# Numbers first, a table in two parts, fewer products of zeros, and other PSUM banks in a fused attention and two-layer kernel

## The chip, the core and the metric

The kernel runs on one core of a Trainium2 chip. The metric is the device time of one execution in microseconds, as the median of three runs. A separate execution is recorded by the hardware profiler; its own time stands beside the median below. The engines are TensorE (PE, matmuls; PEld is its weight load), VectorE (DVE), ScalarE (ACT), GpSimd (POOL) and SyncE (SP), which issues most transfers.

## The reference

Attention over a window with a distance penalty, then two feed-forward layers on the 1536 tokens:

```python
scores = scale * np.matmul(q, k.transpose(0, 1, 3, 2))       # B=2, H=8, S=768, D=64
rel = pos[:, None] - pos[None, :]
is_global = pos[None, :] < int(n_global)                     # 8
is_local = (rel >= 0) & (rel < int(n_local))                 # 96
keep = is_global | is_local
dist = np.where(is_global & ~is_local, float(n_local), np.abs(rel))
scores = np.where(keep, scores + bias, -1e9)                 # bias = -slope[head] * dist
a = softmax(scores)                                          # sum + 1e-9 below the line
x = a @ v                                                    # -> 1536 x 512
h = x @ w_in; g = where(h > 0, h, exp(min(h, 0)) - 1); x = g @ w_out          # 512-2048-512
h = max(x @ w1, x @ w2, x @ w3); out = h @ w_out                              # 512-768-512
```

All arithmetic is in fp32 accuracy. The weights come as 64-bit words that the kernel takes apart, and products run in three parts (high by high, high by low, low by high). `n_global` and `n_local` are inputs, so the table of distances is finished on the chip after they have landed.

## The kernel before

**The steps of the attention.** The work goes in steps of 128 tokens and one pair of heads, two steps to a tile `raw` of queries and keys. A step whose tokens are the first 128 of a sequence has 128 keys, every other one 232. For the first block of 512 tokens the 16 steps run in a loop of `windowed`. In pass k of that loop the following is recorded, and each engine runs its own part in this order (the schedule is manual, nothing is reordered):

- `scores_pe(k)`: PE's scores, L228, into the banks S0 and S1 (k even) or y0 and y1 (k odd)
- in some passes `fill`: products of the identity that nobody reads, L765, into bank h
- `turn_pe(k - 2)`: PE transposes the weights of step k - 2, L298 (128 keys) or L304 (232), into one bank of the ring TX, y2, y3
- `values_pe(k - 3)`: PE's product with v, L327, into the bank that holds the transposes of step k - 3
- `scores_dve(k)`: DVE adds the table of distances `rel` to the scores and takes the minimum, L254, one call per head
- `turn_act(k - 2)`, `scores_act(k)`, `values_high(k - 3)`, `sums(k)`: ACT's copy of the transposes L315, exponentials L275, high part xh L337, sums L237
- `recip(k - 1)`, `norm(k - 1)`: DVE's reciprocal L266 and scaling L288
- `values_low(k - 4)`: DVE's low part xl, L343, the last reader of that step's bank
- from pass 8 on (`CONV`) pieces of the taking apart of the weights, on DVE and ACT

**Ahead of the loop.** PE makes 10 products of zeros (`warm`, L765 with z). POOL writes positions, the scales `qsc` of the queries (8 memsets) and the identity, and scales the queries of each `raw` tile (L198). DVE turns the positions into the table: L152 to L154 before the numbers `ni` are there, L165 to L169 after. SP issues `raw` of pair 0, then `ni`, then pairs 1 and 2.

**Behind the loop.** `begin` starts the feed-forward layer. The first long product `h` is followed by a second one in the same bank, tag h, which waits until DVE's L702 has read the first. Then the outputs y, four tiles in the banks y0 to y3, get eight matmuls with the high part of the activation (`out_high`, L708) and four with the low part (`out_low`, L716). From there on the loop over 16 chunks of the hidden layer fills PE.

Of the kernel before, what the change touches and what calls it, by code (L numbers as in the profile page):

```python
# [12 lines left out]
F32 = mybir.dt.float32  # L13
# [25 lines left out]
BLOCKS = [512, 512, 512]  # L39
CONV = 8  # L40
EARLY = 28
WARM = 10
FILL = {1: 2, 2: 2, 8: 2, 9: 2, 10: 2, 11: 2, 12: 2, 13: 2}
WLOAD = 2, 5, 9, 13
CHUNKS = [(c, i) for c in range(NCC) for i in range(3)]
BEHIND = [(c, i) for c in range(NCC) for i in (0, 2)] + [(c, 1) for c in range(NCC)]
# [3 lines left out]
def load_numbers(nc, pool, n_ap):  # L50
    ni = pool.tile([P, 4], I32, name="ni")
    nc.sync.dma_start(ni, n_ap.bitcast(I32).partition_broadcast(P))
    return ni
# [63 lines left out]
class Windowed:  # L117
# [17 lines left out]
    def positions(self, scratch):  # L135

        nc, c = self.nc, self.const
        n = P + WIN
        rel = c.tile([P, n], F32, name="rel")
        key, neg = scratch[0][:, 0:n], scratch[1][:, 0:n]  # L140
        far = 1 << 20
        o = 0
        for num, step, base, cm, kstep, kbase in (
            (P, -1, 0, 1, 1, 0),
            (PREV, -1, PREV, 1, 0, far),
            (G, 0, far, 0, 1, 0),
            (P, -1, 0, 1, 0, far),
        ):
            iota(nc, rel[:, o:o + num], num, step, base, cm)
            iota(nc, key[:, o:o + num], num, kstep, kbase, 0)  # L150
            o += num
        nc.vector.tensor_scalar(neg, rel, 0.0, None, op0=ALU.is_lt)  # L152
        nc.vector.scalar_tensor_tensor(rel, rel, UNIT, neg, op0=ALU.mult, op1=ALU.max)
        nc.vector.tensor_scalar(key, key, UNIT, None, op0=ALU.mult)  # L154
        self.qsc = query_scales(nc, c, UNIT)
        self.ident = c.tile([P, P], F32, name="ident")
        make_identity(nc, self.ident)
        self.base, self.key, self.tmp = rel, key, neg

    def bases(self, ni):  # L160


        nc, rel, key, t = self.nc, self.base, self.key, self.tmp
        w = self.const.tile([P, 4], F32, name="nu")
        nc.vector.tensor_scalar(w, ni, UNIT, None, op0=ALU.mult)  # L165
        ng, nl = w[:, 0:1], w[:, 2:3]
        nc.vector.tensor_scalar(key, key, ng, nl, op0=ALU.is_ge, op1=ALU.max)
        nc.vector.scalar_tensor_tensor(t, rel, nl, rel, op0=ALU.is_ge, op1=ALU.add)
        nc.vector.tensor_tensor(rel, t, key, op=ALU.min)  # L169
# [229 lines left out]
class Feed:  # L399
# [301 lines left out]
    def elu_max(self, e, h):  # L701
        self.nc.vector.scalar_tensor_tensor(e, e, -1.0, h, op0=ALU.add, op1=ALU.max)  # L702

    def out_high(self, y, fc, g, n):
        w = self.w[fc][:, 1]
        for e in range(NCC):
            for a in range(2):
                self.nc.tensor.matmul(  # L708
                    y[e][:, 0:n], w[:, a, e * P:e * P + P], g[0][:, 0:n],
                    start=fc == 0 and a == 0, stop=False,  # L710
                )

    def out_low(self, y, fc, g, n):
        w = self.w[fc][:, 1]
        for e in range(NCC):
            self.nc.tensor.matmul(  # L716
                y[e][:, 0:n], w[:, 0, e * P:e * P + P], g[1][:, 0:n],
                start=False, stop=fc == NFC - 1,
            )
# [48 lines left out]
    def begin(self, at, k, x, h):  # L768


        copy, n = self.nc.scalar.copy, BLOCKS[0]
        at.load_values(k)
        self.w_ahead(4)
        at.turn_pe(k - 2, "y2")
        at.scores_pe(k, m=2)
        at.recip(k - 1)
        at.norm(k - 1)
        at.turn_pe(k - 1)
        e = self.elu_exp(h, n)
        self.elu_max(e, h)  # L780
        h = self.ps.tile([P, 512], F32, tag="h", name="h")
        self.product(h, self.w[1][:, 0], x, n, order=BEHIND)
        at.turn_act(k - 2, copy)
        self.c_rebase(2)
        at.scores_dve(k)
        self.c_rest(1, 1)
        self.c_low(2)
        gh = self.high(e, n)
        at.turn_act(k - 1, copy)
        at.scores_act(k)  # L790
        at.sums(k)
        self.c_word(2, 0)
        prev = gh, self.low(e, gh, n)
        at.pair_pe(k - 2)
        e = self.elu_exp(h, n)
        self.c_word(2, 1)
        self.elu_max(e, h)
        at.pair_out(k - 2, copy)
        self.c_high(2)
        y = self.out_tiles()  # L800
        self.out_high(y, 0, prev, n)
        self.out_low(y, 0, prev, n)
        at.recip(k)
        at.norm(k)
        gh = self.high(e, n)
        self.c_rebase(3)
        self.c_rest(2)
        gl = self.low(e, gh, n)
        k += 1
        at.turn_pe(k - 1)  # L810
        at.turn_act(k - 1, copy)
        at.scale_queries(k // 2 + 1)
        at.load_pair(k // 2 + 2)
        self.w_ahead(6)
        at.scores_dve(k)
        at.scores_act(k)
        at.sums(k)
        self.c_low(3)
        self.c_word(3, 0)
        at.recip(k)  # L820
        at.norm(k)
        return y, (gh, gl)
# [411 lines left out]
def windowed(tc, ctx, io, flag):  # L1234
# [4 lines left out]
    at.close = own.close  # L1239
    with tc.manual_schedule():  # L1240
        scratch = [f.cv.tile([P, 512], F32, tag="wr", name="sc") for _ in range(2)]
        at.load_pair(0, True)
        f.warm(WARM)
        at.positions(scratch)
        ni = load_numbers(nc, at.const, io["nn"])
        for p in range(1, 3):
            at.load_pair(p, True)
        at.scale_queries(0)
        at.bases(ni)
        first = BLOCKS[0] // GRP * 8  # L1250
        x = f.split_tiles()

        def convert():
            f.c_rebase(0)
            f.c_low(0)
            yield
            f.c_word(0, 0)
            f.c_rebase(1)
            yield
            f.c_word(0, 1)  # L1260
            yield
            f.c_high(0)
            f.c_low(1)
            yield
            f.c_rest(0)
            yield
            f.c_word(1, 0)
            yield
            yield
            f.c_word(1, 1, 0)  # L1270
            yield

        words = convert()
        h = f.ps.tile([P, 512], F32, tag="h", name="h")
        tags = "TX", "y2", "y3"
        for k in range(first):
            e = k % 2
            at.load_values(k, True)
            if e == 0:
                at.load_pair(k // 2 + 3, True)  # L1280
                at.scale_queries(k // 2 + 1)
            at.scores_pe(k, (("S0", "S1"), ("y0", "y1"))[e])
            if k in FILL:
                f.fill(at.ident, FILL[k])
            at.turn_pe(k - 2, tags[k % 3])
            at.values_pe(k - 3)
            if k >= first - 2:
                f.product(h, f.w[0][:, 0], x, GRP, 0, (k - first + 2) * 6, 6)
            at.scores_dve(k, True)
            at.turn_act(k - 2, nc.scalar.copy)  # L1290
            at.scores_act(k)
            at.values_high(k - 3, x)
            at.sums(k)
            at.recip(k - 1)
            at.norm(k - 1)
            at.values_low(k - 4, x)
            if k >= CONV:
                next(words, None)
            if k in WLOAD:
                f.w_load()  # L1300

        def half(first, count):
            f.product(h, f.w[0][:, 0], x, 2 * GRP, GRP, first, count, CHUNKS)

        k = first
        at.load_values(k, True)
        at.load_pair(k // 2 + 3)
        at.scale_queries(k // 2 + 1)
        at.turn_pe(k - 2, tags[k % 3])
        at.values_pe(k - 3)  # L1310
        at.recip(k - 1)
        at.norm(k - 1)
        at.turn_act(k - 2, nc.scalar.copy)
        at.values_high(k - 3, x)
        at.values_low(k - 4, x)
        f.c_word(1, 1, 1)
        f.c_high(1, 0)
        f.c_high(1, 1)
        at.scores_pe(k, m=2)
        at.turn_pe(k - 1, tags[(k + 1) % 3])  # L1320
        at.scores_dve(k, True)
        at.values_low(k - 3, x)
        at.values_pe(k - 2)
        at.turn_act(k - 1, nc.scalar.copy)
        at.values_high(k - 2, x)
        at.scores_act(k)
        at.scores_dve(k + 1, True)
        at.values_low(k - 2, x)
        f.c_rest(1, 0)
        at.values_pe(k - 1)  # L1330
        half(0, 6)
        at.values_high(k - 1, x)
        at.sums(k)
        at.values_low(k - 1, x)
        half(6, 3)
        half(9, 3)
        at.scores_act(k + 1)
        at.sums(k + 1)
        at.recip(k)
        at.norm(k)  # L1340
        for _ in words:
            pass
        begun = f.begin(at, k + 2, x, h)
        f.run(at, first + 4, x, begun, lambda: covered(nc, at.const, ni, flag))
# [100 lines left out]
```

## Time and profile before

| | |
|---|---|
| median of 3 runs | 542.40 us (542.32 to 542.52) |
| profiled execution | 542.16 us, of which the span from first to last instruction is 540.4 us |
| PE busy | 530.4 us, 98% of the span |
| DVE, ACT, POOL busy | 73%, 53%, 15% |

The span is the time between the program's first and last instruction on the core. Busy shares of PE count its matmuls with modelled ends. The views used below are the page's chain of work that ended last, the sums over stretches of time, the timelines of single engines and the list of transfers with the time from issue to landing.

### The profile page before, as it was taken

The numbers are of one execution on the slowest core, as the hardware profiler recorded it, in microseconds if no ns is written. First come the engines' busy times: TensorE is split into PE (matmuls) and PEld (weight loads), VectorE is DVE, ScalarE is ACT, GpSimd is POOL, SyncE is SP. The second block draws the span as 40 slices with busy tenths as digits, with TensorE's granted clock in tenths as the row PEclk, the third lists the DMA queues.
The fourth block names the chain that finished last, engine by engine and source line by source line (L and its number), as shares of the span: only waits on it lengthen the run. The fifth ranks groups of instructions, "written<-read, shape, count | busy, mean of one in ns | idle before, by whom it ended". The sixth has DMA issues, their size and how long they took to land.

```text
span 540.4 us, 7753 instructions
## 1 busy us (share of the span) xinstructions
PE 530.4 (98%) x2746; PEld 427.0 (79%) x2746; DVE 394.1 (73%) x830; ACT 287.9 (53%) x650; POOL 82.9 (15%) x89
## 2 busy tenths in 40 slices
PE   8999999999999999999999999999999999999995
PEld 6667787777777888787888888788888888888884
DVE  6999999999845344443567657688886989779883
ACT  5989877888756555554645565551256321224120
POOL 4210000001000000000000044421035410335000
PEclk9999999999999999999999999999999999999999
DMA  8928255442210111000000031330028301776024
GB/s 295 384 93 329 106 194 196 156 161 84 101 44 24 45 44 44 21 19 1 0 2 0 5 118 35 116 131 26 1 87 301 138 1 45 272 287 234 1 81 159
DMA packets 23455, 59.21 MB, mean 110 GB/s; under 512 B 2416, under 2 KB 2416, under 8 KB 23408
## 3 DMA queue, kind: packets, MB, share of 16 engines
q1 hardware_dynamic: 18368, 49.46, 26.2%
q10 hardware_dynamic: 5040, 9.18, 4.5%
q8 instruction: 24, 0.39, 0.3%
q14 instruction: 23, 0.19, 0.1%
HBM read 49.19 MB, written 9.44 MB: 108 GB/s over the span
## 4 chain that ended last, share of the span: by engine, by line
PE 91%; DVE 4%; ACT 3%; DMA 1%; issue 0%; SPq 0%; DVEq 0%; ACTq 0%
PE h L677 26%; PE y L708 16%; PE y L716 8%; PE y L1027 8%; PE y L1121 5%; PE y L677 5%; PE S L1027 4%; PE TX L327 3%; PE TX L304 3%; PE S L228 2%; PE TX L1027 2%; PE S L1121 2%; PE S L677 2%; PE h L1027 2%; PE TX L1121 2%; ACT p L275 1%
## 5 line engine op out<-in xcount | busy, mean ns | idle before, releaser
L677 PE MATMUL h<-xh,w 128*128 128x512 f32 (+1 forms) x432 | 122.1, 387 | 0.1
L708 PE MATMUL y<-gh,w 128*128 128x512 f32 x384 | 98.8, 399 | 0.1
L513 POOL TENSOR_TENSOR w<-wr,w 128x512 fp32r<-128x512 f32 x42 | 62.9, 1508 | 232.6 <-ACT w L512 230.4
L677 PEld LDWEIGHTS h<-xh,w 128*128 128x128 f32 x432 | 80.2, 188 | 17.3 <-DVE e L702 0.6
L708 PEld LDWEIGHTS y<-gh,w 128*128 128x128 f32 x384 | 69.8, 188 | 14.5 <-issue 0.7
L677 PE MATMUL h<-xl,w 128*128 128x512 f32 (+1 forms) x216 | 71.0, 386 | 0.0
L702 DVE SCALAR_TENSOR_TENSOR e<-e,h 128x512 f32<-128x512 f32 x48 | 32.9, 686 | 50.0 <-ACT e L698 50.0
L512 ACT CAST w<-wr 128x512 fp32r<-128x512 f32 x42 | 27.5, 663 | 63.5 <-DVE wr L503 51.2
L697 ACT ACTIVATE e<-h 128x512 f32<-128x512 f32 x48 | 28.7, 598 | 55.7 <-PE h L677 50.9
L275 ACT ACTIVATE p<-p,m 128x232 f32<-128x232 f32 (+1 forms) x96 | 44.8, 470 | 17.5 <-DVE m L254 17.2
L716 PE MATMUL y<-gl,w 128*128 128x512 f32 x192 | 51.6, 391 | 0.0
L503 DVE SCALAR_TENSOR_TENSOR wr<-wr 128x512 uint32<-128x512 uint32 x48 | 44.3, 923 | 7.4 <-ACT wr L495 6.0
L689 DVE TENSOR_TENSOR gl<-e,gh 128x512 fp32r<-128x512 f32 x48 | 33.1, 690 | 19.9 <-ACT gh L684 19.9
L677 PEld LDWEIGHTS h<-xl,w 128*128 128x128 f32 x216 | 40.4, 188 | 8.1 <-issue 0.2
L198 POOL TENSOR_SCALAR raw<-raw,qsc 128x256 f32<-128x256 f32 x24 | 16.7, 698 | 192.3 <-DMA raw<-qk 178.4
L1027 PE MATMUL y<-t,w 128*128 128x512 f32 x180 | 42.7, 389 | 0.0
L716 PEld LDWEIGHTS y<-gl,w 128*128 128x128 f32 x192 | 36.0, 188 | 7.9 <-issue 0.3
L684 ACT CAST gh<-e 128x512 fp32r<-128x512 f32 x48 | 29.6, 617 | 23.5 <-DVE e L702 23.3
L469 DVE SCALAR_TENSOR_TENSOR wr<-wr 128x1024 uint32<-128x1024 uint32 (+1 forms) x37 | 40.2, 1098 | 0.6
L1027 PEld LDWEIGHTS y<-t,w 128*128 128x128 f32 x180 | 33.8, 188 | 7.0
L698 ACT ACTIVATE e<-e 128x512 f32<-128x512 f32 x48 | 30.3, 632 | 1.5
L1037 ACT CAST g<-m 128x512 fp32r<-128x512 f32 x18 | 10.9, 621 | 35.5 <-DVE m L1056 27.4
(155 smaller groups left out, 837.7 us busy)
## 6 DMA issues: line engine op xcount, KB each, us to landing
wr<-wa SPq DMA_DIRECT2D x14, 1024.0 KB, 6.9
wr<-wb SPq DMA_DIRECT2D x24, 512.0 KB, 4.7
v<-v SPq DMA_DIRECT2D x24, 256.0 KB, 2.8
part<-row ACTq DMA_DIRECT2D x24, 256.0 KB, 4.5
raw<-qk SPq DMA_DIRECT2D x16, 312.0 KB, 4.5
row<-part SPq DMA_DIRECT2D x12, 256.0 KB, 3.1
out<-rows ACTq DMA_DIRECT2D x11, 256.0 KB, 2.8
raw<-qk SPq DMA_DIRECT2D x8, 260.0 KB, 4.7
```

The costliest lines, as they stand in the source:

```text
L275: self.nc.scalar.activation(p[:, o], p[:, o], AF.Exp, bias=m[:, u:u + 1], scale=-1.0, accum_out=m[:, 2 + u:3 + u],)
L469: self.nc.vector.scalar_tensor_tensor(r[..., 0], r[..., 1], v, r[..., 0], op0=op, op1=ALU.bitwise_or)
L503: self.nc.vector.scalar_tensor_tensor(t, a, c, t, op0=op, op1=ALU.bitwise_or)
L513: nc.gpsimd.tensor_tensor(w[:, u, 1], v, w[:, u, 0].bitcast(F32), op=ALU.subtract)
L677: nc.tensor.matmul(out[:, o:n], w[:, part % 2, c * P:c * P + P], (xl if part == 2 else xh)[:, c, o:n], start=(c, part) == order[0], stop=( ...
L689: (engine or self.nc.vector).tensor_tensor(gl[:, 0:n], e[:, 0:n], gh[:, 0:n].bitcast(F32), op=ALU.subtract)
L698: self.nc.scalar.activation(e, e, AF.Exp, scale=-1.0)
L702: self.nc.vector.scalar_tensor_tensor(e, e, -1.0, h, op0=ALU.add, op1=ALU.max)
L708: self.nc.tensor.matmul(y[e][:, 0:n], w[:, a, e * P:e * P + P], g[0][:, 0:n], start=fc == 0 and a == 0, stop=False,)
L716: self.nc.tensor.matmul(y[e][:, 0:n], w[:, 0, e * P:e * P + P], g[1][:, 0:n], start=False, stop=fc == NFC - 1,)
L1027: self.nc.tensor.matmul(out, w[:, u, i % 2, b + c * P:b + c * P + P], o[:, i // 2, c], start=c == i == 0, stop=c == 1 and i == 2,)
L1121: nc.tensor.matmul(o, t[:, a, r], w[:, u, b], start=u == k == 0, stop=u == 1 and k == 2,)
```

## The change

The loads: SP issues `ni` ahead of `raw` of pair 0. On POOL the scaling of pair 0 comes right after the scales, ahead of the identity.

The products of zeros: 7 ahead of the loop in place of 10, two more products of the identity in pass 0, and in pass 8 the two stand behind `values_pe` instead of ahead of `turn_pe`.

The table: `bases` takes a slice of columns. It is called for the first 128 columns (those of steps with 128 keys) ahead of the loop, and for the other 232 in pass 0 behind `scores_dve(0)`.

The banks: `turn_pe` in passes 2 to 5 takes TX, y2, y3 and h; the other passes keep the ring of three. In `begin` the second long product takes the bank y3 in place of h. The outputs y0 to y2 get their high and low matmuls first, and y3 its own behind them.

```diff
-WARM = 10
-FILL = {1: 2, 2: 2, 8: 2, 9: 2, 10: 2, 11: 2, 12: 2, 13: 2}
+WARM = 7
+FILL = {0: 2, 1: 2, 2: 2, 8: 2, 9: 2, 10: 2, 11: 2, 12: 2, 13: 2}
...
-    def bases(self, ni):
-        nc, rel, key, t = self.nc, self.base, self.key, self.tmp
+    def take_numbers(self, ni):
         w = self.const.tile([P, 4], F32, name="nu")
-        nc.vector.tensor_scalar(w, ni, UNIT, None, op0=ALU.mult)
-        ng, nl = w[:, 0:1], w[:, 2:3]
+        self.nc.vector.tensor_scalar(w, ni, UNIT, None, op0=ALU.mult)
+        self.nu = w[:, 0:1], w[:, 2:3]
+
+    def bases(self, o):
+        nc = self.nc
+        rel, key, t = (a[:, o] for a in (self.base, self.key, self.tmp))
+        ng, nl = self.nu
...
-        h = self.ps.tile([P, 512], F32, tag="h", name="h")
+        h = self.ps.tile([P, 512], F32, tag="y3", name="h")
         self.product(h, self.w[1][:, 0], x, n, order=BEHIND)
...
-        self.out_high(y, 0, prev, n)
-        self.out_low(y, 0, prev, n)
+        for rows in range(NCC - 1), (NCC - 1,):
+            self.out_high(y, 0, prev, n, rows)
+            self.out_low(y, 0, prev, n, rows)
...
+        ni = load_numbers(nc, at.const, io["nn"])
         at.load_pair(0, True)
         f.warm(WARM)
         at.positions(scratch)
-        ni = load_numbers(nc, at.const, io["nn"])
+        at.qsc = query_scales(nc, at.const, UNIT)
         for p in range(1, 3):
             at.load_pair(p, True)
         at.scale_queries(0)
-        at.bases(ni)
+        at.ident = at.const.tile([P, P], F32, name="ident")
+        make_identity(nc, at.ident)
+        at.take_numbers(ni)
+        at.bases(slice(0, P))
...
         tags = "TX", "y2", "y3"
+        rings = {2: "TX", 3: "y2", 4: "y3", 5: "h"}
...
-            if k in FILL:
+            if k in FILL and k != CONV:
                 f.fill(at.ident, FILL[k])
-            at.turn_pe(k - 2, tags[k % 3])
+            at.turn_pe(k - 2, rings.get(k, tags[k % 3]))
             at.values_pe(k - 3)
+            if k == CONV:
+                f.fill(at.ident, FILL[k])
...
             at.scores_dve(k, True)
+            if k == 0:
+                at.bases(slice(P, P + WIN))
```

The order of the instructions shows three places. The first is DVE's start, from the reading of the numbers (`nu`) on; `sc` and `rel` are the table, ISA rows with `p,m` are L254 (L256 in the changed program). Before:

```order
L165 TENSOR_SCALAR nu<-ni 128x4
L167 TENSOR_SCALAR sc<-sc,nu 128x360
L168 SCALAR_TENSOR_TENSOR sc<-rel,nu 128x360
L169 TENSOR_TENSOR rel<-sc 128x360
L254 ISA p,m<-S_151,rel 128x128
L254 ISA m 128x1
L254 ISA p,m<-S_152,rel 128x128
L254 ISA m 128x1
L254 ISA p,m<-y_162,rel 128x232
```

And changed:

```order
L169 TENSOR_SCALAR sc<-sc,nu 128x128
L170 SCALAR_TENSOR_TENSOR sc<-rel,nu 128x128
L171 TENSOR_TENSOR rel<-sc 128x128
L256 ISA p,m<-S_148,rel 128x128
L256 ISA m 128x1
L256 ISA p,m<-S_149,rel 128x128
L256 ISA m 128x1
L169 TENSOR_SCALAR sc<-sc,nu 128x232
L170 SCALAR_TENSOR_TENSOR sc<-rel,nu 128x232
L171 TENSOR_TENSOR rel<-sc 128x232
L256 ISA p,m<-y_165,rel 128x232
```

Three passes over the 232 columns now stand between the minima of step 0 and those of step 1.

The second place is PE in passes 5 to 7. Names with `ident` are transposes, those with `v` the product with v; the number at a tile tells which one it is. Before:

```order
L304 MATMUL y3_263<-ident_126,p_218 116x128 x4
L327 MATMUL y2_239<-p_194,v_179 64x128 x2
L228 MATMUL S0_290<-raw_148 128x128
L228 MATMUL S1_291<-raw_148 128x128
L298 MATMUL TX_294<-ident_126,p_246 128x128 x2
L327 MATMUL y3_263<-p_218,v_179 64x128 x4
L228 MATMUL y0_314<-raw_148 128x232
L228 MATMUL y1_315<-raw_148 128x232
L304 MATMUL y2_318<-ident_126,p_270 116x128 x4
```

And changed:

```order
L306 MATMUL h_266<-ident_130,p_221 116x128 x4
L329 MATMUL y3_242<-p_197,v_182 64x128 x2
L230 MATMUL S0_293<-raw_145 128x128
L230 MATMUL S1_294<-raw_145 128x128
L300 MATMUL TX_297<-ident_130,p_249 128x128 x2
L329 MATMUL h_266<-p_221,v_182 64x128 x4
L230 MATMUL y0_317<-raw_145 128x232
L230 MATMUL y1_318<-raw_145 128x232
L306 MATMUL y2_321<-ident_130,p_273 116x128 x4
```

The transposes of step 3 go into h where they went into y3; y3 was step 0's bank before. Those of step 5 follow into y2, which in the changed program was step 1's bank and before was step 2's.

The third place is PE in `begin`, behind the second long product. Before:

```order
L327 MATMUL TX_706<-p_655,v_607 64x128 x4
L708 MATMUL y_762<-gh_736,w_467 128x512 x2
L708 MATMUL y_763<-gh_736,w_467 128x512 x2
L708 MATMUL y_764<-gh_736,w_467 128x512 x2
L708 MATMUL y_765<-gh_736,w_467 128x512 x2
L716 MATMUL y_762<-gl_743,w_467 128x512
L716 MATMUL y_763<-gl_743,w_467 128x512
L716 MATMUL y_764<-gl_743,w_467 128x512
L716 MATMUL y_765<-gl_743,w_467 128x512
```

And changed:

```order
L329 MATMUL TX_709<-p_658,v_610 64x128 x4
L710 MATMUL y_765<-gh_739,w_470 128x512 x2
L710 MATMUL y_766<-gh_739,w_470 128x512 x2
L710 MATMUL y_767<-gh_739,w_470 128x512 x2
L718 MATMUL y_765<-gl_746,w_470 128x512
L718 MATMUL y_766<-gl_746,w_470 128x512
L718 MATMUL y_767<-gl_746,w_470 128x512
L710 MATMUL y_768<-gh_739,w_470 128x512 x2
L718 MATMUL y_768<-gl_746,w_470 128x512
```

The two high matmuls of the last tile, y3, have moved behind the three low ones of the others.

## Rows read from the trace of the kernel before

**Rows 1.** The page's chain of work that ended last, by engine.
```profile
PE 91%; DVE 4%; ACT 3%; DMA 1%; issue 0%; SPq 0%; DVEq 0%; ACTq 0%
```

**Rows 2.** Stretches: us, then busy time of each engine, granted clock, DMA share, GB/s.
```profile
core 0: us, PE busy (x) PEld busy (x) DVE busy (x) ACT busy (x) POOL busy (x), PEclk, DMA share, GB/s
1.00:5.00 4.00, 4.00 (x19) 4.00 (x20) 1.87 (x6) 1.01 (x1) 3.28 (x19) 1.00 0.69 170
...
20.00:30.00 10.00, 9.80 (x84) 6.78 (x81) 9.86 (x38) 10.00 (x33) 2.58 (x4) 1.00 0.83 305
45.00:540.00 495.00, 488.99 (x2417) 397.07 (x2415) 356.45 (x672) 251.30 (x520) 71.84 (x54) 1.00 0.27 95
```

**Rows 3.** Timeline, DVE, 4 to 8 us: start, duration, operation, [idle before, releaser].
```profile
4.45 0.47 DVE L167 TENSOR_SCALAR sc<-sc,nu 128x360 f32<-128x360 f32 x1
...
5.45 0.53 DVE L169 TENSOR_TENSOR rel<-sc 128x360 f32<-128x360 f32 x1
6.14 0.29 DVE L254 CUSTOM_DVE_ANT_0 p<-S,rel 128x128 f32<-128x128 f32 x1 [0.15 <-PE S L228]
...
6.57 0.40 DVE L254 CUSTOM_DVE_ANT_0 p<-y,rel 128x232 f32<-128x232 f32 x1
...
7.21 0.08 DVE L254 DVE_READ_ACCUMULATOR2_ANT m<- 128x1 f32 x1
7.62 0.17 DVE L266 RECIPROCAL m<-m 128x2 f32<-128x2 f32 x1 [0.33 <-ACT m L237]
```

**Rows 4.** Timeline, DVE and PE, 12 to 14 us.
```profile
12.14 0.59 DVE L288 TENSOR_SCALAR p<-p,m 128x232 f32<-128x232 f32 x2
12.65 0.29 DVE L343 TENSOR_TENSOR xl<-y,xh 128x128 fp32r<-128x128 f32 x1
...
13.08 0.62 PE L304 MATMUL y<-ident,p 128*116 128x128 f32 x4 [0.66 <-DVE xl L343]
```

**Rows 5.** First two transfers: queue, count, KB, us from issue to landing.
```profile
raw<-qk SPq DMA_DIRECT2D x1, 260.0 KB, 2.9
...
ni<-nn SPq DMA_DIRECT2D x1, 2.0 KB, 3.0
```

**Rows 6.** Timeline, SP's issues and POOL, 0 to 5 us.
```profile
0.73 0.40 SPq L190 DMA_DIRECT2D raw<-qk  x1
...
1.19 0.42 SPq L52 DMA_DIRECT2D ni<-nn  x1
...
2.20 1.38 POOL L110 MEMSET qsc<- 64x1 f32 x8
...
4.20 0.48 POOL L198 TENSOR_SCALAR raw<-raw,qsc 128x256 f32<-128x256 f32 x1
```

**Rows 7.** PE's start: timeline to 8.5 us, and L765 by form (min/median/max ns).
```profile
0.98 4.58 PE L765 MATMUL z<-z 128*128 128x128 f32 x20 [0.98 <-POOL z L759]
5.49 0.49 PE L228 MATMUL S<-raw 64*128 64x128 f32 x4
...
8.16 0.52 PE L298 MATMUL y<-ident,p 128*128 128x128 f32 x2
...
L765 PEld LDWEIGHTS z<-ident x32: 186/190/193, 6.3 to 29.9; 128*128 128x128 f32 x32
...
L765 PEld LDWEIGHTS z<-z x20: 288/333/334, 1.0 to 5.0; 128*128 128x128 f32 x20
```

**Rows 8.** Timeline, ACT, 7 to 18 us.
```profile
7.50 0.47 ACT L275 ACTIVATE p<-p,m 128x232 f32<-128x232 f32 x1
...
13.74 0.58 ACT L315 COPY p<-y 116x512 f32<-116x512 f32 x1 [0.54 <-PE y L304]
...
17.36 0.58 ACT L315 COPY p<-y 116x512 f32<-116x512 f32 x1 [0.54 <-PE y L304]
```

**Rows 9.** Timeline, PE, ACT and DVE in `begin`, 45 to 51 us.
```profile
45.36 0.19 PEld L677 LDWEIGHTS h<-xh,w 128*128 128x128 f32 x1 [0.35 <-DVE e L702]
...
49.18 0.60 ACT L697 ACTIVATE e<-h 128x512 f32<-128x512 f32 x1 [0.92 <-DVE gl L689]
...
49.33 2.11 PE L708 MATMUL y<-gh,w 128*128 128x512 f32 x8
...
50.48 0.69 DVE L702 SCALAR_TENSOR_TENSOR e<-e,h 128x512 f32<-128x512 f32 x1 [0.26 <-ACT e L698]
```

More of the change, by code (lines that the diff above doesn't have):

```diff
@@ L154, in positions @@
         nc.vector.tensor_scalar(key, key, UNIT, None, op0=ALU.mult)
-        self.qsc = query_scales(nc, c, UNIT)
-        self.ident = c.tile([P, P], F32, name="ident")
-        make_identity(nc, self.ident)
         self.base, self.key, self.tmp = rel, key, neg
-    def bases(self, ni):
-        nc, rel, key, t = self.nc, self.base, self.key, self.tmp
+    def take_numbers(self, ni):
         w = self.const.tile([P, 4], F32, name="nu")
-        nc.vector.tensor_scalar(w, ni, UNIT, None, op0=ALU.mult)
-        ng, nl = w[:, 0:1], w[:, 2:3]
+        self.nc.vector.tensor_scalar(w, ni, UNIT, None, op0=ALU.mult)
[4 more added lines that the diff above has]
+        ng, nl = self.nu
         nc.vector.tensor_scalar(key, key, ng, nl, op0=ALU.is_ge, op1=ALU.max)
@@ L702, in elu_max, with out_high @@
         self.nc.vector.scalar_tensor_tensor(e, e, -1.0, h, op0=ALU.add, op1=ALU.max)
-    def out_high(self, y, fc, g, n):
+    def out_high(self, y, fc, g, n, rows=range(NCC)):
         w = self.w[fc][:, 1]
-        for e in range(NCC):
+        for e in rows:
             for a in range(2):
@@ L711, in out_high, with out_low @@
                 )
-    def out_low(self, y, fc, g, n):
+    def out_low(self, y, fc, g, n, rows=range(NCC)):
         w = self.w[fc][:, 1]
-        for e in range(NCC):
+        for e in rows:
             self.nc.tensor.matmul(
```

## The prediction

> **What bounds the kernel now.** I read the chain of work that ended last first. Summed over the run it is TensorE (PE) for 91% [rows 1], and from 45 us to the end PE is busy in 489.0 of 495 us [rows 2]. Nothing after 45 us can be shortened by this change, except by handing PE its work earlier. So I read the timeline of the first 45 us, where the attention of the first 512 tokens is made in 16 steps. A step has PE's scores S, DVE's biased minimum L254, ACT's exponentials L275 and sums L237, DVE's reciprocal L266 and scaling L288, PE's transposes, ACT's copy L315, PE's product with v, and the two halves xh (ACT) and xl (DVE) of its result. The pace is set first by the landing of the numbers ni and the table of distances on DVE, done at 5.98 us [rows 3]; then by ACT and DVE in turn, with two waits of PE for xl that ACT inherits [rows 4, 8]; and then by DVE alone, which from 20 to 30 us is busy for 9.86 of 10 us [rows 2]. What is won before 20 us therefore arrives whole at PE's first long products, as long as nothing else holds DVE back. None of the waits in these rows from 12 us on is for a transfer.
>
> **The change part by part: numbers loaded first.** SP issues the first query and key tile (raw of pair 0) at 0.73 us and ni at 1.19 [rows 6], and they landed 2.9 and 3.0 us later [rows 5]. The swap puts ni at 0.73 + 3.0 = 3.73 and pair 0 at 1.19 + 2.9 = 4.09 us: the table gains 0.46 us, the scores lose 0.46. For the scores this costs nothing, since POOL was not waiting for pair 0. It had memsets of the query scales to 2.20 + 1.38 = 3.58 and the identity ahead of the scaling at 4.20, which ends at 4.68 [rows 6]. With the identity moved behind it, the scaling runs from 4.14 to 4.62, where it was.
>
> **Fewer products of zeros.** The 20 passes (10 products of two) take PE from 0.98 to 5.49 us [rows 7], 0.226 each; 14 end at 4.14. The first scores can then start at about 4.65, when the scaling is done, 0.84 earlier than at 5.49. How fast they run there hangs on the clock. The granted clock reads 1.00 also from 1 to 5 us [rows 2], the 2.4 GHz level, but the durations do not agree: a weight load of the same form takes 333 ns on z up to 5.0 us and 190 ns on the identity from 6.3 us on [rows 7], a factor of 1.75, so PE was at the lower level (1.2 GHz) until 5.0 us at least, having run without a gap since 0.98. I price the scores at 4.65 at that factor: 0.49 [rows 7] becomes 0.86, done at 5.51, and DVE's first L254 starts at about 5.6 instead of 6.14 [rows 3]. The two new products after these scores wait for the identity (about 5.2 us) and lie under the table's second part, so I cost them at nothing; without that cover they are 4 passes, 0.5 us.
>
> **The table in two parts.** The first 128 columns are ready at about 3.73 + 0.2 + 0.9 = 4.8 us, before the scores at 5.6. The two L254 of step 0 take 0.43 (6.14 to 6.57 [rows 3]), to 6.03. Then come the other 232 columns, ahead of step 1's L254. A pass over 360 columns took 0.53 us (L169 [rows 3]) and the same operation over 128 columns 0.29 (L343 [rows 4]): 1.03 ns a column. The three passes took 1.53 us (4.45 to 5.98), so over 232 columns they take 1.53 - 3 x 128 x 1.03 ns = 1.13, and with the 0.15 us between the table and the first L254 [rows 3] 1.28. Step 1's L254 starts at 7.31 instead of 6.57, 0.74 later: only step 0 is helped. What is left of that: ACT's exponentials of step 1 started at 7.50, behind those of step 0 [rows 8]; now, 0.43 behind their L254, at 7.74, 0.24 later. DVE's reciprocal of step 0 started at 7.62 after waiting 0.33 us [rows 3]; now it queues behind 0.64 us of L254 (6.57 to 7.21 [rows 3]) and starts at 7.98, 0.36 later. At the reciprocal of step 1, which needs ACT's sums and DVE's queue, the two meet at 0.25 later. So the start **costs 0.25**. Bounds: if pair 0 lands at 3.63 as it did, the scaling and all behind it are 0.46 earlier, a gain of 0.2; if it lands 0.2 later than I have it, a cost of 0.45.
>
> **Four banks.** The transposed tile of a step holds its bank until that step's xl. With three banks the transposes of step 3 wait 0.66 us for DVE's xl of step 0 and start at 13.08 [rows 4], and ACT, which has nothing else, sits idle 0.54 us before the copy at 13.74; the same comes again 3.62 us later, before the copy at 17.36 [rows 8]. With h as the fourth, the bank is free a whole step earlier and the transposes wait for the scaling L288 alone, done at 12.73 [rows 4]. What is late next is ACT's own queue, which is free at 13.74 - 0.54 = 13.20. If the first half of the transposes run while DVE scales the second half, the copy starts there, a gain of 0.54; if all four wait for the second half, they start at about 12.77, the copy 0.66 later at 13.43, a gain of 0.31. The changed program waits for DVE at the first and again at the third of them, which is the former; I take 0.5 for each of the two, **a gain of 1.0**, bounds 0.6 and 1.08. From step 9 on the ring is of three again, but there DVE sets the pace. For the same reason the products of zeros of step 8, now behind the transposes, give nothing: the copy they free runs beside DVE's queue.
>
> **Another bank, and outputs by rows.** PE is idle 0.35 us before the second long product at 45.36, until DVE's L702 of the first has freed bank h [rows 9]. In y3 the product can start some 0.3 earlier. But y3 is then held until L702 of that product ends at 51.17, and this one does not move with PE: ACT's L697 before it waits 0.92 us for DVE's gl [rows 9]. With the rows 0 to 2 first, PE has nine matmuls of (2.11 - 0.5) / 7 = 0.23 us from 49.33 - 0.3 on [rows 9] and comes to y3 at 51.1, waits to 51.2, and pays perhaps 0.1 for the restart. Net **a gain of 0.15**, bounds 0 and 0.35.
>
> **Sum.** 0.25 - 1.0 - 0.15 = -0.9 us. The profiled execution took 542.16 us, 540.4 of it span, so 1.76 lie outside and stay; it would come to 541.26. It is 0.24 below the median of the three runs, 542.40, which would come to **541.5**.
>
> **The rivals.** *Clock late.* PE has a gap from 4.14 to 4.65 and short ones behind it, where before it had none. If the higher level is granted only near 9 us, PE's work between the first scores and the first transposes (5.49 to 8.16 us [rows 7], some 2.3 of it work, and 0.5 for the new products) takes 1.75 times as long, 4.9 us from 4.65: the transposes come at 9.5, not at 8.16 + 0.36. With what follows in the next step that is about 1.2 us, net 542.7. For it speaks that the only rise the rows show came after four us without a gap; against it, that the passes on the identity keep to 190 ns up to 29.9 us [rows 7], through waits like that at 13.08. The Trainium skill (TensorE: Matmul & The Clock Gate, Part 1) says that "the default state is throttled, and activity releases the throttle", which speaks against taking activity away here; how much may go, no run shows yet.
>
> *Clock very late, the slower side.* The same mechanism at a higher price: two steps last 3.62 us [rows 8], most of it work of PE, so a rise only after 12 us adds some 1.5 us more: 544.2. It decides for slower from a rise later than about 10 us.
>
> *Pair 0 not late.* If ni takes no time in the queues that pair 0 would notice, pair 0 lands at 3.63 us or little later and the start gains 0.2 in place of costing 0.25: 541.0; with both other terms at their good ends 540.8. Against it: ni, 2 KB, took 3.0 us like the tile of 260 KB [rows 5], so it does not cost by its size. [...]
>
> *The fourth bank does nothing.* If the waits at steps 3 and 5 end by something beside xl, only 0.25 - 0.15 is left: 542.5.
>
> **How the numbers follow.** Forecast (541.5, own range 541.0 to 542.0) 0.60; pair 0 not late (541.0) 0.18; clock late or no use of the bank (542.6) 0.14; clock very late (544.2) 0.08. 0.2% of 542.4 is 1.08 us, about what can be told from no change: faster is below 541.3, slower above 543.5. Faster: a third of the forecast's case and nearly all of the second, 0.37. Slower: the last case and a remainder of the third, 0.09. The rest is 0.54. The range reaches from the second case's good end, 540.8, to the third's bad one, 542.8.
>
> **What would show it.** The first L254 at 5.6 us, step 1's at 7.3, the reciprocal of step 0 near 8.0; no wait for xl at steps 3 and 5 and no idle 0.54 us of ACT; weight loads of 128 columns at 190 ns from 5.4 us on; the second long product within 0.1 us of the transposes, and a short wait before y3's matmuls. Wrong would be: a scaling of pair 0 before 4.0 us, weight loads of 333 ns after 6 us, or a new wait of PE for the bank h.

## The result, and the profile after

| | kernel before | changed kernel |
|---|---|---|
| median of 8 runs each, side by side | 542.36 us (541.96 to 542.56) | 546.13 us (541.79 to 549.46) |
| profiled execution, and its span | 542.16, 540.4 us | 546.57, 544.7 us |
| DVE's two L702 (after: L704) of the first long products | 44.62, 50.48 us | 49.55, 55.41 us |

The ratio is 1.0064, with a 95% interval of 1.0044 to 1.0084: slower, where 541.5 was forecast with "slower" at 0.09. One run of the eight, 541.79, is where the forecast put it; the spread, 7.7 us against 0.6 before, is part of the result. The intervals here leave out a kernel's runs that lie over 1.5% above its fastest; the counts of late runs below take in every run.

The whole loss is there by the first long products. The two L704 are 4.93 us later than the L702 of before, and the profiled run is 4.41 longer, so some 0.5 us was won back behind them. The first of each pair, before and changed:

```profile
44.62 0.69 DVE L702 SCALAR_TENSOR_TENSOR e<-e,h 128x512 f32<-128x512 f32 x1 [0.36 <-ACT e L698]
```

```profile
49.55 0.69 DVE L704 SCALAR_TENSOR_TENSOR e<-e,h 128x512 f32<-128x512 f32 x1 [0.35 <-ACT e L700]
```

The timeline of the changed kernel's DVE, 3 to 9.5 us, answers to [rows 3] (start, duration, engine, line, operation, [idle before it, and what ended it]):

```profile
3.62 0.17 DVE L160 TENSOR_SCALAR nu<-ni 128x4 f32<-128x4 int32 x1 [0.33 <-DMA ni<-nn]
...
4.46 0.29 DVE L171 TENSOR_TENSOR rel<-sc 128x128 f32<-128x128 f32 x1
6.25 0.29 DVE L256 CUSTOM_DVE_ANT_0 p<-S,rel 128x128 f32<-128x128 f32 x1 [1.49 <-PE S L230]
...
8.48 0.40 DVE L256 CUSTOM_DVE_ANT_0 p<-y,rel 128x232 f32<-128x232 f32 x1 [0.60 <-PE y L230]
...
9.12 0.16 DVE L268 RECIPROCAL m<-m 128x2 f32<-128x2 f32 x1
```

The table's first part is ready at 4.75, and nobody can use it: DVE idles 1.49 us for the scores. The first two transfers and POOL's scaling say why, answering to [rows 5, 6] (queue, count, KB, us from issue to landing; then the timelines of SP's queue and of POOL):

```profile
raw<-qk SPq DMA_DIRECT2D x1, 260.0 KB, 3.5
ni<-nn SPq DMA_DIRECT2D x1, 2.0 KB, 2.9
```

```profile
0.74 0.40 SPq L52 DMA_DIRECT2D ni<-nn  x1
1.19 1.37 SPq L192 DMA_DIRECT2D raw<-qk  x3
```

```profile
4.88 0.48 POOL L200 TENSOR_SCALAR raw<-raw,qsc 128x256 f32<-128x256 f32 x1 [1.30 <-DMA raw<-qk]
```

Pair 0 took 3.5 us behind ni, not 2.9, landed at 1.19 + 3.5 = 4.7, and POOL waited 1.30 us for it. Now PE, answering to [rows 7]: the timeline, and L767 by form between 6 and 19 us (min/median/max ns). The view begins inside the products of zeros, so its first row counts only the last nine of their 14 passes.

```profile
2.22 2.13 PE L767 MATMUL z<-z 128*128 128x128 f32 x9
5.42 0.80 PE L230 MATMUL S<-raw 64*128 64x128 f32 x4 [1.08 <-POOL raw L200]
6.15 1.22 PE L767 MATMUL z<-ident 128*128 128x128 f32 x4
...
14.57 0.80 PE L230 MATMUL S<-raw 64*128 64x128 f32 x4
...
18.05 1.11 PE L306 MATMUL h<-ident,p 128*116 128x128 f32 x4
...
19.66 0.49 PE L230 MATMUL S<-raw 64*128 64x128 f32 x4
```

```profile
L767 PEld LDWEIGHTS z<-ident x12: 286/333/333, 6.1 to 10.8; 128*128 128x128 f32 x12
```

The products of zeros end at 4.35, PE has nothing for 1.08 us, and then four score matmuls of the same form take 0.80 at 5.42 and at 14.57, but 0.49 at 19.66. The weight loads on the identity stay at 333 ns, where [rows 7] had 190. The clock's own records, from which the granted clock is made, begin in this execution at 19.56 us, and in that of before at 5.36. So PE was at 1.2 GHz, the lower of its two levels, until 19.56. The stretches, answering to [rows 2], add that this was not for want of work:

```profile
5.40:19.50 14.10, 14.08 (x64) 9.13 (x64) 8.09 (x44) 7.22 (x31) 3.33 (x8) 1.00 0.88 340
20.00:30.00 10.00, 10.00 (x86) 6.60 (x83) 9.21 (x43) 9.91 (x38) 1.06 (x3) 1.00 0.92 315
```

PE is busy in 14.08 of 14.10 us. The granted clock, the column behind POOL's, reads 1.00 there too; ahead of the first record that column tells nothing, and the durations have to be read. The scores of steps 0 and 6 lie 14.24 us apart (5.42 and 19.66), against 8.51 in before (5.49 and 14.00): 5.7 us lost, of which 4.93 are left at the L704. Step 6 in the kernel before:

```profile
14.00 0.49 PE L228 MATMUL S<-raw 64*128 64x128 f32 x4
```

ACT at steps 3 and 5 and PE in `begin` answer to [rows 8, 9]:

```profile
14.05 0.58 ACT L317 COPY p<-y 116x512 f32<-116x512 f32 x1 [0.73 <-PE y L306]
...
19.19 0.58 ACT L317 COPY p<-h 116x512 f32<-116x512 f32 x1 [1.73 <-PE h L306]
```

```profile
49.54 0.41 PEld L306 LDWEIGHTS TX<-ident,p 128*116 128x116 f32 x4 [0.29 <-DVE p L290]
49.92 0.19 PEld L679 LDWEIGHTS h<-xh,w 128*128 128x128 f32 x1
```

ACT still waits, though not for a bank: PE has no gap ahead of the transposes, and they take 1.11 us instead of the 0.62 of [rows 4]. The second long product follows the transposes at once, without the 0.35 us of [rows 9]. The chain of work that ended last, by engine, answering to [rows 1], is PE's still more:

```profile
PE 93%; DVE 3%; ACT 2%; DMA 1%; issue 0%; POOL 0%; SPq 0%; POOLq 0%; ACTq 0%
```

### The profile page after: what moved, and what is told of

It reads as the page before. It is cut to its first block, busy times and chain, and to the rows that moved or that the text cites. A ratio compares the mean times of both kernels' runs of the same rounds, so it can differ in the third digit from the quotient of the medians.

```text
span 544.7 us, 7755 instructions
## 1 busy us (share of the span) xinstructions
PE 535.7 (98%) x2744; PEld 429.5 (79%) x2744; DVE 394.2 (72%) x833; ACT 288.3 (53%) x650; POOL 82.7 (15%) x89
## 4 chain that ended last, share of the span: by engine, by line
PE 93%; DVE 3%; ACT 2%; DMA 1%; issue 0%; POOL 0%; SPq 0%; POOLq 0%; ACTq 0%
PE h L679 27%; PE y L710 16%; PE y L718 8%; PE y L1030 7%; PE y L1124 4%; PE y L679 4%; PE S L1030 4%; PE S L230 3%; PE TX L329 3%; PE TX L306 3%; PE S L1124 2%; PE TX L1030 2%; PE S L679 2%; PE h L1030 2%; PE TX L1124 1%; PE y L230 1%
## 5 line engine op out<-in xcount | busy, mean ns | idle before, releaser
L704 DVE SCALAR_TENSOR_TENSOR e<-e,h 128x512 f32<-128x512 f32 x48 | 32.9, 686 | 50.0 <-ACT e L700 49.7
L256 DVE CUSTOM_DVE_ANT_0 p<-S,rel 128x232 f32<-128x232 f32 (+1 forms) x80 | 26.8, 372 | 4.0 <-PE S L230 3.9
```

## The experiments

Theory A: the clock is late because PE had too little to do ahead of the first scores, in products or in the gap behind them. Theory B: the table in two parts, or pair 0's landing, costs the time by itself. Theory C: the other bank and the rows make a new wait. Fourteen kernels were run, each beside runs of the kernel before.

**The changed kernel with 10 products of zeros.**

```diff
-WARM = 7
+WARM = 10
```

> The changed kernel with 10 products of zeros ahead of the loop in place of 7; all else as changed. Theory A (clock: with 7 products PE's clock rises late, at 19.6 us in the profiled run, and at another time in each run): weight loads of 128 columns at 190 ns from about 5.4 us, runs within 0.6 us of each other, and the rest of the change is left, worked out with pair 0 landing at 4.8 us: start +0.8, four banks -1.0, bank y3 -0.15, so 542.0. Theory B (the table in two parts and the later pair 0 are what costs): still 545 or more, with the spread. Theory C (the fourth bank h or y3 makes a new wait): still 545 or more.

Measured: 541.90 (541.32 to 542.46), before 542.49, ratio 0.999 [0.9981, 0.9999]. PE's timeline, again from inside the products of zeros:

```profile
2.21 2.70 PE L767 MATMUL z<-z 128*128 128x128 f32 x15
5.40 0.49 PE L230 MATMUL S<-raw 64*128 64x128 f32 x4 [0.49 <-POOL raw L200]
```

The clock's first record is at 4.01 us. Pair 0 is as late and the table still in two parts, yet three more products of zeros take back 4.2 us. The scores start at the same time and take 0.49. B and C are out as the main cause.

**The kernel before with 7 products.**

```diff
-WARM = 10
+WARM = 7
```

> The kernel before with 7 products of zeros in place of 10, nothing else. Theory A: the clock rises late here too, PE's rows double in length beyond 8 us, median 544 to 548 with several us between runs. Theories B and C: within 0.3 us of 542.4, since PE is not what the first step waits for (the table is done at 5.98 us).

Measured: 542.26 (541.67 to 545.6), ratio 1.0013 [0.9996, 1.0029]. Three of 11 runs lie at 544.9 to 545.6, the others with before. In the profile, of a run of 541.74, the clock rose at 4.28 and PE's gap ahead of the scores is 0.39 us. So 7 products alone make only some runs late; A has to hold the gap too.

**The changed kernel with 10 products and the table in one piece.**

```diff
-WARM = 7
+WARM = 10
-at.bases(slice(0, P))
+at.bases(slice(0, P + WIN))
-            if k == 0:
-                at.bases(slice(P, P + WIN))
```

> The changed kernel with 10 products of zeros and the table of distances made in one piece ahead of the loop; numbers first and the banks as changed. Theory A: early clock, and without the second part of the table ahead of step 1 the start costs nothing: -1.0 -0.15 -0.1, 541.2; against the run with 10 products and the table in two parts 0.8 less. Theory B gives the same here and is told from A by that run. Theory C: 545 or more.

Measured: 541.76 (541.23 to 542.21), ratio 0.9987 [0.9978, 0.9996], not to be told from the 541.90 with two parts, where 0.8 less was expected. Step 1's L256 was at 7.86 with two parts, and in one piece it is hardly earlier, though the table is ready:

```profile
7.63 0.40 DVE L256 CUSTOM_DVE_ANT_0 p<-y,rel 128x232 f32<-128x232 f32 x1 [0.82 <-PE y L230]
```

DVE waits 0.82 us for PE's scores of step 1, which stand behind the two new products of the identity (6.29 to 6.93). So with the table in one piece those scores, and not the table, hold step 1 up; no run leaves the two products out. PE's gap is 0.74 us here, but the clock had risen at 4.27, ahead of it, and stayed: the scores at 5.77 take 0.49.

**The kernel before with the ring of four, bank y3 and the rows.**

```diff
+rings = {2: "TX", 3: "y2", 4: "y3", 5: "h"}
-at.turn_pe(k - 2, tags[k % 3])
+at.turn_pe(k - 2, rings.get(k, tags[k % 3]))
-h = self.ps.tile([P, 512], F32, tag="h", name="h")     # in begin
+h = self.ps.tile([P, 512], F32, tag="y3", name="h")
+for rows in range(NCC - 1), (NCC - 1,):                # out_high, out_low by rows
```

(and the products of zeros of pass 8 behind its transposes)

> The kernel before with the banks alone: the ring of four in passes 2 to 5, the second long product in y3, the outputs by rows, the products of pass 8 behind the product with v; 10 products of zeros, table and loads as before. Theories A and B: no wait for xl at steps 3 and 5, 541.2 to 541.5. Theory C: slower than 542.4.

Measured: **541.42** (540.66 to 541.86), before 542.49, ratio 0.9979 [0.997, 0.9988], the best of all kernels here. ACT's copies of steps 3 and 5 and PE in `begin`:

```profile
13.35 0.59 ACT L315 COPY p<-h 116x512 f32<-116x512 f32 x1
...
16.63 0.59 ACT L315 COPY p<-y 116x512 f32<-116x512 f32 x1 [0.20 <-PE y L304]
```

```profile
43.80 0.41 PEld L304 LDWEIGHTS TX<-ident,p 128*116 128x116 f32 x4 [0.29 <-DVE p L288]
44.18 0.19 PEld L677 LDWEIGHTS h<-xh,w 128*128 128x128 f32 x1
```

Of the two waits of 0.54 of [rows 8] the first is gone and the second is down to 0.20, and the 0.35 of [rows 9] is gone. L702 is at 43.81, 0.81 earlier than before.

**The changed kernel with pair 0 first.**

```diff
-        ni = load_numbers(nc, at.const, io["nn"])
         at.load_pair(0, True)
+        ni = load_numbers(nc, at.const, io["nn"])
```

> The changed kernel with its first two transfers in the old order (raw of pair 0, then ni); 7 products of zeros and all else stay. Theory A (what keeps PE at 1.2 GHz to 19.56 us is the stretch in which PE has nothing between the last product of zeros at about 4.05 us and the first scores, 1.4 us long because raw of pair 0 lands at 4.85): the scaling runs at 4.2 to 4.7 as before, PE's gap is about 0.7 us, the clock rises before 6 us in most runs, median 541.5 to 542.5, with perhaps a third of the runs 2 to 4 us later, as in the run of the kernel before with 7 products. Rival (7 products are too few with the first 128 columns of the table first, whatever the gap): 545 to 547, the clock rising after 12 us.

Measured: 542.19 (540.96 to 550.77), ratio 1.0014 [0.9988, 1.004]. Pair 0 takes 2.9 us again, its scaling is at 3.78, sooner than expected, and PE goes from the zeros to the scores without a gap:

```profile
2.22 2.13 PE L767 MATMUL z<-z 128*128 128x128 f32 x9
4.32 0.80 PE L230 MATMUL S<-raw 64*128 64x128 f32 x4
5.05 1.14 PE L767 MATMUL z<-ident 128*128 128x128 f32 x4
6.12 0.66 PE L230 MATMUL y<-raw 64*128 64x232 f32 x4
```

The clock rose at 5.97 in this execution, within the third row. Seven of 12 runs lie at 540.96 to 542.30, five at 544.2 to 550.8. Without the gap 7 products are enough in most runs, not in all.

**The numbers from ACT's queue** (10 products, table whole, pair 0 first on SP).

```diff
-    nc.sync.dma_start(ni, ...)
+    nc.scalar.dma_start(ni, ...)
```

> The changed kernel with 10 products of zeros, the table in one piece, and the numbers issued from ACT's queue while SP issues raw of pair 0 first: so the banks and the rows stay, and neither transfer stands behind the other. My theory (the late landing of pair 0 is the price of standing behind ni in SP's queue): both land at 3.6 to 3.9 us, the scaling is at about 4.2, the first L254 at 5.6 to 6.0, median 541.0 to 541.4. Rival (the two transfers share the DMA engines, and ni delays pair 0 from any queue): pair 0 at 4.4 or later, the first L254 at 6.1 to 6.3, median 541.6 to 541.9 as with ni first on SP and the table whole.

Measured: 542.40 (541.72 to 543.05), ratio 1.0004 [0.9995, 1.0013]. My theory failed. Of the rival only the late pair 0 came (4.4 us or later), not its time: both transfers got slower.

```profile
5.03 0.19 DVE L160 TENSOR_SCALAR nu<-ni 128x4 f32<-128x4 int32 x1 [1.70 <-DMA ni<-nn]
```

```profile
5.03 0.49 POOL L200 TENSOR_SCALAR raw<-raw,qsc 128x256 f32<-128x256 f32 x1 [1.53 <-DMA raw<-qk]
```

The numbers landed 4.3 us after issue and pair 0 4.1, both are used from 5.03 on, and the first L256 is at 7.29. A second queue does not separate the two; why both are late was not followed further.

**The kernel before with 4 products** (WARM = 4).

> The kernel before with 4 products of zeros in place of 10, nothing else. Theory A (the stretch without products ahead of the first scores decides the clock; 8 passes end at about 2.8 us and the scores start at 4.7, so it is 1.9 us): nearly all runs have the clock late, 544 to 548 us, L702 at 47 to 50 us. Rival (the number of products has little to do with it; what makes the changed kernel late is its table or its first transfers): 542 to 543 as with 7 products, only a part of the runs later.

Measured: 544.76 (543.75 to 548.49), ratio 1.0071 [1.0043, 1.0099], all six runs late; in the profile, of a run of 543.84, the gap is 1.67 us and the clock rises at 11.92. As A has it.

**The kernel before with the table in two parts alone.** (`bases` cut as in the change.)

> The kernel before with only the table of distances in two parts (128 columns, then 232 behind the first two L254); 10 products of zeros, pair 0 first, banks as before. My theory (step 1's minimum stands behind the second part): step 0's L254 starts at 5.5 to 5.9, step 1's at 7.3 to 7.7 instead of 6.57, the reciprocal of step 0 at 8.0 to 8.4 instead of 7.62, and the run is 0.3 to 0.8 us longer, 542.7 to 543.2. Rival (the earlier first minimum is kept, the second part fills a wait of DVE): 541.9 to 542.4, step 2 on at the times of before or earlier.

Measured: 543.15 (542.34 to 545.18), before 542.37, ratio 1.002 [1.0012, 1.0029]. DVE:

```profile
6.03 0.29 DVE L259 CUSTOM_DVE_ANT_0 p<-S,rel 128x128 f32<-128x128 f32 x1 [0.36 <-PE S L233]
...
6.46 0.59 DVE L172 TENSOR_SCALAR sc<-sc,nu 128x232 f32<-128x232 f32 x1
...
7.99 0.40 DVE L259 CUSTOM_DVE_ANT_0 p<-y,rel 128x232 f32<-128x232 f32 x1
...
8.63 0.16 DVE L271 RECIPROCAL m<-m 128x2 f32<-128x2 f32 x1
```

Step 0 gains 0.11 (6.03 against 6.14), step 1 loses 1.42 (7.99 against 6.57) and the reciprocal 1.01 (8.63 against 7.62). The three rows are 0.1 to 0.3 us later than the latest that I expected, the time is inside the expected range: the medians differ by 0.78. Two of the 11 runs took 544.03 and 545.18.

**The changed kernel with its 7 products later** (z's memset behind POOL's IOTAs).

```diff
-        f.warm(WARM)
         at.positions(scratch)
+        f.warm(WARM)
```

> The changed kernel with the memset of z moved behind POOL's ten IOTAs, so that its 7 products of zeros run from about 2.4 to 5.5 us instead of 0.97 to 4.05; all else stays, pair 0 still behind ni. The first scores can start at 5.4 (scaling 4.88 to 5.36), so PE has no gap ahead of them, with the same 7 products. Theory A (the gap of 1.4 us ahead of the scores makes the clock late): the clock rises before 7 us, the first L256 at about 6.0 to 6.4, median 541.6 to 542.3, as with 10 products from 0.97 us. Rival (7 products are too few, the gap has no part in it): the clock late, 545 to 547.

Measured: 542.78 (541.90 to 551.14), ratio 1.0013 [1.0001, 1.0025]. The products run from 2.52 to 5.88 and the scores follow at 5.81. Eight of 12 runs lie at 541.9 to 542.8, four at 544.9 to 551.1; the profile is of one of the four, with the clock at 14.75. Pair 0 is as late as in the changed kernel and the products are as many, only later: closing the gap in this way took 7 late runs of 8 down to 4 of 12.

**The kernel before with the scores held back** behind 10 products.

```diff
+        for _ in range(11):
+            nc.gpsimd.memset(self.ident, 0.0)
         make_identity(nc, self.ident)
```

> The kernel before with 11 more memsets of the identity's tile on POOL ahead of the scaling (about 0.2 us each, 2.2 in all); its 10 products of zeros stay and end at 5.5. The first scores start at about 6.9 instead of 5.5, so PE has a gap of 1.4 us behind 10 products. Theory A (a gap of this length makes the clock late, whatever was ahead of it): the clock rises after 9 us in most runs, L702 at 47 us or later, 544.5 to 549. Rival (10 products are enough and the gap costs only itself): the clock rises by about 5 us or soon after the scores, the first L254 at about 7.5 instead of 6.14, L702 at 45.5 to 46, 543.0 to 543.8.

Measured: 547.19 (544.99 to 550.84), ratio 1.0094 [1.0066, 1.0121], gap 2.21 us in place of the planned 1.4, clock at 20.35.

**The same with 15 products**, meant to fill the gap.

> The kernel before with the 11 memsets of e10_scores_late (scores not before about 7.8 us) and 15 products of zeros instead of 10, which end at about 7.8, so PE has no gap ahead of the scores. If the gap was what made the clock late there: the clock rises at 4 to 6 us, the first L254 at 8.2 to 8.4, and the cost is the later start alone, L702 at 46 to 47, 543.5 to 545.0. Rival (the late scores themselves, or the memsets on POOL, cost the 5 us): 546 to 548 again.

Measured: 544.22 (543.75 to 545.03), before 542.56, ratio 1.0032 [1.0019, 1.0044]. The scores start at the same time in both:

```profile
7.84 0.80 PE L230 MATMUL S<-raw 64*128 64x128 f32 x4 [2.21 <-POOL raw L200]
```

```profile
7.85 0.49 PE L230 MATMUL S<-raw 64*128 64x128 f32 x4 [1.46 <-POOL raw L200]
```

The first row is of the kernel with 10 products, the second of that with 15. There the clock rose at 4.78, the products ended sooner than I had reckoned, at 6.4, and a gap of 1.46 did not bring it down. Scores 2.4 us later cost 1.66 by themselves; the 3 us beyond that, with 10 products, go with the late clock.

**With 7 memsets instead of 11**, 10 products.

> The kernel before with 7 such memsets: the scaling at about 6.2, the first scores at 6.7, so a gap of 1.1 us behind 10 products that end at 5.6, as long as that of the changed kernel behind 7. If the gap alone decides: most runs late, 544.5 to 548. If the number of products counts as much (with 10 of them the clock has mostly risen before they end): most runs with the clock at 4 to 5.5, the first L254 at 7.1 to 7.3, 542.8 to 543.5, a few late.

Measured: 544.38 (542.71 to 550.33), ratio 1.0053 [1.002, 1.0086]. Pair 0's scaling came at 6.38 and the clock rose at 3.94, so the products ended at 4.88 and the gap is 2.02 us, longer than planned: the question of a gap of 1.1 behind 10 products stays open. Eight of the 10 runs took more than 543.6, with scores 1.4 us later than before in any case. But this profile shows what a gap can do to a clock that has risen. The stretches (us, busy time and count of PE, PEld, DVE, ACT, POOL, granted clock) and PE's timeline:

```profile
4.00:7.30 3.30, 1.28 (x14) 1.08 (x15) 1.69 (x4) 0.00 (x0) 2.88 (x11) 1.00 0.96 327
7.40:14.10 6.70, 6.70 (x30) 4.24 (x28) 4.46 (x25) 3.97 (x17) 1.83 (x4) 0.50 1.04 412
14.20:20.00 5.80, 5.07 (x46) 3.05 (x44) 4.19 (x23) 5.26 (x26) 1.12 (x2) 1.00 0.99 347
```

```profile
6.91 0.49 PE L230 MATMUL S<-raw 64*128 64x128 f32 x4 [2.02 <-POOL raw L200]
7.23 0.87 PE L230 MATMUL y<-raw 64*128 64x232 f32 x4
8.03 1.22 PE L767 MATMUL z<-ident 128*128 128x128 f32 x4
```

The clock had risen, PE had nothing from 4.88 to 6.91, the clock fell at 7.36, half a microsecond after PE was at work again, and stayed down to 14.18 while PE was busy in 6.70 of 6.70 us.

**The ring of four alone** on the kernel before.

> The kernel before with only the ring of four banks for the transposes of passes 2 to 5 and the fill of pass 8 behind the transposes. My prediction gave this part 1.0 us of the 1.15 of all three: 541.2 to 541.6, L702 at 43.7 to 44.0, no wait of ACT for an L317 product over 0.3 us between 12 and 18 us. Rival (the gain seen with all three is in the other bank and the rows): 542.1 to 542.4, L702 at 44.5 or later.

Measured: 541.49 (541.03 to 542.42), before 542.21, ratio 0.9985 [0.9976, 0.9994]. The two waits of ACT are gone, that of 0.34 for L702 in `begin` is still there. L702 is at 44.65, not at the expected 43.7 to 44.0, in a profiled run of 542.42, the longest of the 11.

**Bank y3 and the rows alone.**

> The kernel before with only the second product's bank y3 in place of h and the first outputs by rows. My prediction gave this 0.15 us (0 to 0.35): 542.0 to 542.4, the second product starting behind the transposes without the wait of 0.35 for L702, and a wait ahead of the outputs of row 3 of at most 0.2. Rival (more than half of the gain of all three is here): 541.4 to 541.8.

Measured: 542.00 (541.60 to 542.77), ratio 0.9997 [0.9988, 1.0006], 0.21 by the medians, which the interval does not tell from nothing. ACT's two waits of 0.54 are back, the second product starts at 45.48 behind transposes at 45.09, and no wait shows ahead of the matmuls of row 3. C is out.

**All of it by products and gap.** The slowest of 114 runs of the kernel before beside these kernels took 543.52 us; a run over 543.6 is counted late.

| kernels | products of zeros | PE's gap ahead of the scores in the profile, us | late runs |
|---|---|---|---|
| before | 10 | none | 0 of 114 |
| six with early scores | 10 | 0 to 0.74 | 0 of 66 |
| before with the table in two parts | 10 | none | 2 of 11 |
| pair 0 first; 7 on before; 7 later | 7 | 0, 0.39, 0.23 (weight loads) | 5 of 12, 3 of 11, 4 of 12 |
| the changed kernel | 7 | 1.08 | 7 of 8 |
| 4 on before | 4 | 1.67 | 6 of 6 |

The table in two parts has a median of 543.15 by itself, near the bound; whether the clock was late in its two runs no profile shows. The three kernels with added memsets are left out, since their late scores cost time by themselves.

## Why the prediction was wrong

**The step that failed is the clock, which the sum puts at nothing.** The forecast takes weight loads at 190 ns from 5.4 us on; a later rise stands only among the rivals, "clock very late" with a chance of 0.08. In the changed kernel the rise came at 19.56, and with three more products of zeros, a rise at 4.01 and all else the same it took 541.90 in place of 546.13: the term left out is 4.2 us. The rival's mechanism was named, and the sign listed for it, weight loads of 333 ns after 6 us, is the one that came. Its price did not fit as well: I had 544.2, 2.7 over the forecast, for a rise after 12 us. The kernel before with 4 products, in a run of 543.84 with a rise at 11.92, lost 1.5 against its 542.37; the changed kernel, with its rise later still, lost more. I gave the rival little because "the passes on the identity keep to 190 ns up to 29.9 us [rows 7], through waits like that at 13.08". Those rows show a clock that has already risen and keeps up through a short wait; so do the gaps of 0.74 and 1.46 us above. They say nothing on one that has yet to rise. In the change PE stopped at 4.35, and where 10 products or more ran from 0.98 us on, the rise came at 3.94 to 7.13 (that of the 2.21 us gap aside): 7 products end inside that spread. The sentence quoted from the Trainium skill (TensorE: Matmul & The Clock Gate, Part 1), that activity releases the throttle, was the better guide than the rows I set against it; the run in which the clock falls at 7.36 behind a gap agrees. That PE was busy for 14.08 of 14.10 us without a rise does not agree, if all work of PE is taken as activity, and there the measurement decides.

**Numbers loaded first** fed it. ni took 2.9 us, 0.1 less than forecast, but pair 0 took 3.5 instead of 2.9, landed at 4.7 instead of 4.09, and its scaling began at 4.88 instead of 4.14. "For the scores this costs nothing" fell with that: scores at 5.42, not 4.65, and the gap, forecast at 0.5, became 1.08. With pair 0 first the gap is nil and the median 542.19. My bound, a landing 0.2 later, was too narrow; all I had to set it was one duration of a transfer that ran alone ahead of the others.

**Fewer products of zeros**: the two new ones I costed at nothing "under the table's second part". They take 1.22 us at the lower clock, not 0.5, and step 1's scores start behind them at 7.30; step 1's L256 is at 8.48, DVE having waited 0.60 for those scores. At the higher clock they cost too: the wait of 0.82 with the table in one piece is for scores behind them.

**The table in two parts**: direction right, size short. Step 1's L254 was forecast at 7.31 and the start's cost at 0.25. Alone on the kernel before the cut puts it at 7.99 and costs 0.78 (ratio 1.0012 to 1.0029). The working let the table start 0.5 earlier, and without that the second part begins at 6.46 instead of 6.03. For both edits at the higher clock, the changed kernel with 10 products (541.90) against the banks alone (541.42) gives 0.48, where I had 0.25 with a bound of 0.45. Of the 0.48 the cut is 0.14 by the medians (541.90 against 541.76 in one piece), which the spread of the runs does not tell from nothing.

**Four banks, another bank, rows**: right. Forecast 1.0 + 0.15 = 1.15, measured 542.49 - 541.42 = 1.07. The ring alone gave 0.72, inside the bounds of 0.6 and 1.08 but short of the 1.0 that I took; the rest gave 0.21 by the medians where I had 0.15, not to be told from nothing. The wait for y3 that I priced at 0.1 is not there.

One reading was wrong without harm. I wrote that from 20 to 30 us the pace is set "by DVE alone", at 9.86 of 10 us; the same row of [rows 2] has ACT busy for 10.00 and PE for 9.80. What was won before 20 us still arrived: 0.81 at the first L702 with all the banks changed.

So where its assumption on the clock holds the sum has the right sign and two thirds of its size: -0.9 forecast, -0.59 with 10 products, 541.90, inside the range of the forecast's own case. The changed kernel gave back some 4.2 us through three products that did no work.

**What stays open**: why some runs with 7 products and no gap rise early and others late; whether 10 products with a gap of 1.1 us would be late; and why PE, busy throughout with scores, transposes and products on the identity, went 14 us without a rise.

## What to carry to other kernels

Before taking dummy products out of a start, find in several profiles when the clock rises, and let neither these products end nor a gap begin well ahead of the rises seen. PE being busy is not enough by itself: here it was busy for 14 us at the lower clock. Three products fewer and a gap of 1.08 us cost 4.2 us here, and one profile or one median hides it: look at the spread of the runs. A small transfer put ahead of a large one on the same queue delayed its landing by 0.6 us here; price that by a row of two transfers behind each other, or leave the order alone.

## What was not expected of the hardware

- The clock rose at 4.01, 4.04, 4.27, 4.61, 4.77, 5.36, 5.40 and 7.13 us in the profiles of eight kernels whose 10 products all start at 0.98 or 0.99 us.
- At the lower level PE was busy 14.08 of 14.10 us without a rise (5.40 to 19.50), and 6.70 of 6.70 (7.40 to 14.10).
- The 260 KB of pair 0 landed 2.6 to 2.9 us after issue with ni behind it on the same queue, 3.5 behind the 2 KB of ni; with ni on ACT's queue both came later than in any other order, pair 0 4.1 and ni 4.3 us after issue.
